# Changing the cost model of a software-scheduled transformer kernel: SyncE charges, GpSimd multiplies, gated PV terms and early fill

## The chip, the cores and the metric

The kernel runs on one core of one Trainium2 chip. The metric is the device time of one execution in microseconds (us), as the median of several executions. Smaller is better.

Names of engines, with what this kernel has them do: PE multiplies matrices, ScalarE (ACT) applies activation functions, VectorE (DVE) and GpSimd (POOL) do elementwise work, and SyncE (SP) issues the transfers, one after another: in the timeline of its queue after the change, from 626.17 to 633.66 us, each begins only when the one before it has ended.

## The reference, cut to what matters

```python
# S = 2048 tokens, D = 512, F = 1792, H = 32 heads of Dh = 16
def _A_ref(x, wqkv, wo):                      # attention
    qkv = ...; q, k, v = qkv[0], qkv[1], qkv[2]
    scores = jnp.einsum("bhqd,bhkd->bhqk", q, k) * Dh ** -0.5
    p = _softmax(scores, axis=-1)
    o = jnp.einsum("bhqk,bhkd->bhqd", p, v)
    return o.transpose(...).reshape(B, S, D) @ wo
def _B_ref(x, w1, w2):                        # feed-forward
    return _silu(x @ w1) @ w2
x = x + _A_ref(_layernorm(x), A_wqkv, A_wo);  x = x + _B_ref(_layernorm(x), B_w1, B_w2)
x = x + _A_ref(_layernorm(x), A_wqkv, A_wo);  x = x + _B_ref(_layernorm(x), B_w1, B_w2)
```

There are 32 heads with 2048 x 2048 scores in each of two layers, so the exponentials dominate: they take 1468.6 of the 1513.8 us for which ScalarE is busy (page below).

## The kernel before

The kernel is a stream of steps. Each step computes four 128x512 blocks of scores. ScalarE exponentiates three of them exactly (one activation of 512 columns and one of 1024), and VectorE and GpSimd approximate the fourth: VectorE converts the scores to a bit pattern (`d_y`), and GpSimd makes two more terms (`d_z`) from it. The rest, the *background* (projections, normalisations `xn`, feed-forward), is cut into parts, and a scheduler written in Python puts each part into a step where a model of the engines says it will fit without making ScalarE wait. The order of instructions on each engine is fixed when the kernel is built. A wrong number in the model is therefore never corrected at run time: it becomes a wait.

```python
class Model:                                   # (cut)
    GROUP = 0.217;  FIX = 0.69;  TRANSPOSE = 1.27;  TRANSPOSED = 1.7;  DMA = 0.64
    def transpose(self):                       # a transposing transfer on SyncE's queue
        self.sp = max(self.sp, self.dve + 0.1) + self.TRANSPOSE
        self.landed = self.sp + self.TRANSPOSED
    def fits(self, cost, landed=0.0):
        held, pe, dve, sums, _ = cost
        if landed > (self.pe if pe else self.dve):
            return False
        ...
```

A part names what it needs (`need=("xn", ...)`: one of three buffers that a transpose must have read; `need=("fT", L, c)`: transposed tiles), and the model's `landed` time decides when it may be placed. The feed-forward loads its weights two tiles ahead and names no need for them:

```python
    class W1:                                  # (cut)
        def get(self, ft):
            self.load(ft + 2)                  # one dma_start on SyncE; w1pool has 3 buffers
            if bg.model: bg.model.dma(1)
            return self.tiles.pop(ft)
```

The output of a head group is divided by its sum; where it came by a transposing transfer, both inputs are in SBUF. The model charges 0.43 us of VectorE time:

```python
        nc.vector.reciprocal(rec[:], att[:, :, :, 16:17])
        yield part(0.43, held=not by_dma(L, qc, pi, g, par))
        nc.vector.tensor_tensor(out=attn[L, qc]..., in0=att[:, :, :, 0:DH],
                                in1=rec[:].to_broadcast([P, 4, 4, DH]), op=ALU.mult)
```

*Fill* is matmul work without use (`zero` weights into an open accumulator, or `warm` into a free bank), put into PE's gaps and meant to keep its clock up, which in the trace of before fell to half after windows in which PE was busy for 2.13 and 1.00 of 3.4 us (windows view below).

The softmax here doesn't subtract the row's maximum and nothing guards it: scores larger than these inputs give would overflow.

## Time and profile before

| | before |
|---|---|
| median of 3 executions | 1565.61 us (1565.21 to 1566.28) |
| span of the profiled execution | 1562.4 us |
| before the first exponential | 14.1 us |
| stream of exponentials and tanhs, if ScalarE never waited | 1494.5 us |
| ScalarE's waits in the stream | 13.1 us |
| after the last exponential | 40.9 us |

The third to sixth rows are my own arithmetic on the trace: I took the ends of successive ScalarE activations. When nothing waits, an end follows the end before it by 490 ns (512 columns) or 917 ns (1024 columns); what is above that, counted where it exceeds 60 ns, is a stall. The four parts add up to the span within 0.3 us. (The prediction's 13.8 us also counts 0.65 us before the stream.)

First the page of the kernel before: the busy table, then two groups (line, engine, operation, output and inputs, count, busy us, mean ns, idle before it and its releaser).

```profile
PE 1474.8 (94%) x13400; PEld 468.1 (30%) x13400; DVE 1079.3 (69%) x1733; ACT 1513.8 (97%) x2191; POOL 1114.4 (71%) x1184
...
L1157 ACT ACTIVATE p_sb<-s_ps 128x512 bf16<-128x512 f32 x2026 | 1468.6, 1105 | 9.3 <-PE d_ps L925 8.2
...
L619 DVE TENSOR_TENSOR attn<-ot,rec 128x256 bf16<-128x256 bf16 x45 | 49.4, 1098 | 1.5
```

ScalarE is busy for 97% of the span, nearly all of it in exponentials. The mean of 1105 ns is not the time that one adds: activations overlap in the trace (2026 of 1105 ns are 2239 us, within 1468.6 us busy), which is why I used the ends. The VectorE multiply (the second group) has a mean of 1098 ns, where the model charges 430. The tile view of `attn` shows minimum, median and maximum in ns:

```profile
L619 DVE TENSOR_TENSOR attn<-ot,rec x45: 425/1274/1291, 235.6 to 1506.9; 128x256 bf16<-128x256 bf16 x45
...
L619 DVE TENSOR_TENSOR attn<-att,rec x19: 411/424/425, 172.2 to 1523.9; 128x256 bf16<-128x256 f32 x19
```

The same multiply takes 424 ns if one input is in PSUM (second line) and mostly 1274 ns if both are in SBUF (first line). Not always: seven of the 45 took 425 to 432 ns. In this trace, six of these began when at most 0.16 us was left of the GpSimd instruction that was running (a `d_z`), and one when GpSimd was idle; each of the other 38 ended 268 to 275 ns after the running `d_z` did. So in this trace the slow multiply ends with GpSimd's running instruction, as if it waited for it; it is not slow in itself.

The waits view of the kernel before (who waited for whom: us in total, times, longest) and its timeline near 250 us (start, us, engine, line, operation; in brackets the idle time before it and what ended it) belong together:

```profile
ACT p_sb L1157 <- PE d_ps L925: 8.2, 10, 3.0
...
PE d_ps L925 <- DVE d_y L1074: 7.1, 9, 3.1
...
DVE xn L414 <- DMA fT<-xn: 4.3, 2, 4.1
```

```profile
246.69 5.58 SPq L317 DMA_TRANSPOSE fT<-xn  x3
...
250.63 0.42 DVE L414 TENSOR_SCALAR xn<-x,mv,rstd 128x513 bf16<-128x513 bf16 x1 [4.13 <-DMA fT<-xn]
250.96 0.68 DVE L1074 TENSOR_SCALAR d_y<-d_ps 128x512 uint16<-128x512 f32 x1
251.70 0.37 PE L925 MATMUL d_ps<-QT,KT 32*128 32x512 bf16 x1 [3.15 <-DVE d_y L1074]
...
253.44 1.51 ACT L1157 ACTIVATE p_sb<-s_ps 128x512 bf16<-128x512 f32 x2 [3.00 <-PE d_ps L925]
```

VectorE could not write the normalised tile before 250.63, because SyncE's queue had not finished the transpose that reads its buffer. It held up the `d_y` behind it for 4.13 us, PE waited 3.15 us for that, and ScalarE resumed only at 253.44. With 1.0 us more in the half-clock spell that follows, this place costs ScalarE 4.1 us.

The last view that matters is the windows view of the kernel before: a stretch, its length, busy time of PE, its weight loads, VectorE, ScalarE and GpSimd (x instructions), then the granted PE clock (1.00 is full), DMA share and GB/s.

```profile
30.90:34.30 3.40, 2.13 (x18) 0.40 (x14) 3.34 (x9) 3.06 (x5) 1.29 (x4) 1.00 0.01 3
34.30:44.50 10.20, 8.45 (x45) 1.21 (x47) 7.06 (x14) 8.25 (x12) 6.97 (x8) 0.50 0.43 105
...
249.30:252.70 3.40, 1.00 (x13) 0.23 (x12) 1.61 (x3) 1.15 (x2) 0.00 (x0) 1.00 0.54 112
252.70:256.10 3.40, 3.40 (x20) 0.79 (x20) 1.60 (x4) 1.75 (x3) 2.09 (x2) 0.50 0.03 6
```

PE runs at half clock from 34.3 to 44.5 us and from 252.7 to 256.1 us. Before both, PE's work was thin: 2.13 of 3.4 us busy, and 1.00 of 3.4. Two further half-clock spells (stretches in which half the clock is granted), at 85.5 and 1051.5 us, are 3.4 us long.

### The profile page before, as it was taken

How to read it: one execution, taken by the hardware profiler on the slowest of the kernel's cores; microseconds unless marked ns; L12 is line 12 of the kernel's file. 1: busy time of each engine (PE TensorE's matmuls, PEld its weight loads, DVE VectorE, ACT ScalarE, POOL GpSimd, SP SyncE). 2: the span in 40 equal slices, each digit the busy share in tenths (PEclk: the TensorE clock that was granted, in tenths of full speed). 3: DMA queues.
4: the chain of work that ended last, by engine and by line, in shares of the span. 5: the costliest groups of instructions: out<-in, count | busy, mean ns of one | idle time of the engine just before them, and what ended most of it. 6: DMA issues, size and time to landing. Idle time of an engine off the chain costs nothing. (4 is left out here: it accounts for less than half of the span.)

```text
span 1562.4 us, 34354 instructions
## 1 busy us (share of the span) xinstructions
PE 1474.8 (94%) x13400; PEld 468.1 (30%) x13400; DVE 1079.3 (69%) x1733; ACT 1513.8 (97%) x2191; POOL 1114.4 (71%) x1184
## 2 busy tenths in 40 slices
PE   7999998899999999899998999998999899999998
PEld 3222332232322322222322323322332232222225
DVE  6877676667776777767776677676667666676645
ACT  6999998999999999999999999999999999999993
POOL 2888776677876778667876778776777677776760
PEclk9999999999999999999999999999999999999999
DMA  4110023101221112201122010121022101121110
GB/s 142 28 28 2 5 39 62 31 18 42 45 45 28 31 25 49 52 17 41 21 47 45 11 35 8 25 58 32 18 46 62 30 19 29 45 48 22 39 45 14
DMA packets 149443, 55.85 MB, mean 36 GB/s; under 512 B 127776, under 2 KB 148768, under 8 KB 149280
## 3 DMA queue, kind: packets, MB, share of 16 engines
q1 hardware_dynamic: 149280, 53.65, 15.0%
q8 instruction: 105, 1.72, 0.5%
q14 instruction: 58, 0.48, 0.1%
HBM read 28.57 MB, written 4.19 MB: 21 GB/s over the span
## 5 line engine op out<-in xcount | busy, mean ns | idle before, releaser
L1157 ACT ACTIVATE p_sb<-s_ps 128x512 bf16<-128x512 f32 x2026 | 1468.6, 1105 | 9.3 <-PE d_ps L925 8.2
L1074 DVE TENSOR_SCALAR d_y<-d_ps 128x512 uint16<-128x512 f32 x1012 | 696.9, 689 | 400.5 <-PE d_ps L925 359.5
L925 PE MATMUL s_ps<-QT,KT 32*128 32x512 bf16 x3084 | 629.8, 383 | 51.6 <-ACT p_sb L1157 38.8
L925 PE MATMUL d_ps<-QT,KT 32*128 32x512 bf16 x1012 | 390.1, 385 | 10.3 <-DVE d_y L1074 7.1
L925 PEld LDWEIGHTS <-KT 32*128 32x128 bf16 x4096 | 186.8, 91 | 639.9 <-issue 587.1
L949 PE MATMUL o_ps<-p_sb,VA 128*32 128x512 bf16 x3039 | 311.8, 388 | 8.2 <-DVE oB L1054 1.1
L949 PE MATMUL o_ps<-d_y,VA 128*32 128x512 f16 x1012 | 153.2, 379 | 0.0
L949 PEld LDWEIGHTS <-VA 128*32 128x32 bf16 x4096 | 86.7, 95 | 161.6 <-issue 123.8
L727 PE MATMUL f_ps<-w_sb,hT 128*128 128x512 bf16 x392 | 104.1, 382 | 0.0
L949 PEld LDWEIGHTS <-VB 128*32 128x32 f16 x2024 | 78.3, 98 | 55.6 <-issue 0.8
L949 PE MATMUL o_ps<-w_qkv,zero 128*32 128x512 bf16 x1344 | 93.1, 382 | 0.0
L665 ACT ACTIVATE t_sb<-h_ps 128x512 f32<-128x512 f32 x98 | 88.1, 899 | 0.0
L668 DVE SCALAR_TENSOR_TENSOR hT<-t_sb,h_ps 128x512 bf16<-128x512 f32 x98 | 67.2, 686 | 22.8 <-ACT t_sb L665 22.6
L619 DVE TENSOR_TENSOR attn<-ot,rec 128x256 bf16<-128x256 bf16 x45 | 49.4, 1098 | 1.5
L1054 DVE CAST oT<-o_ps 128x512 bf16<-128x512 f32 x64 | 43.5, 680 | 7.7 <-PE o_ps L949 7.7
L414 DVE TENSOR_SCALAR xn<-x,mv,rstd 128x513 bf16<-128x513 bf16 x64 | 41.6, 663 | 5.7 <-DMA fT<-xn 4.3
L403 DVE BATCH_NORM_STATS2 st<-x 128x6 f32<-128x512 bf16 x64 | 43.5, 680 | 2.0 <-DMA x<-in_A_x_dram 2.0
L727 PEld LDWEIGHTS <-hT 128*128 128x128 bf16 x392 | 29.3, 98 | 46.4 <-issue 25.0
L949 PEld LDWEIGHTS <-zero 128*32 128x32 bf16 x1344 | 25.5, 95 | 40.3 <-issue 28.1
L480 PE MATMUL k_ps<-xnT,w_qkv 128*128 128x512 bf16 x128 | 35.4, 389 | 1.6 <-DVE xnT L444 0.9
L480 PE MATMUL q_ps<-xnT,w_qkv 128*128 128x512 bf16 x136 | 36.6, 389 | 0.0
L407 POOL TENSOR_SCALAR rstd<-mv 128x2 f32<-128x2 f32 x32 | 7.7, 240 | 39.4 <-DVE mv L405 37.9
(2299 smaller groups left out, 2109.1 us busy)
## 6 DMA issues: line engine op xcount, KB each, us to landing
wo<-in_A_wo_dram SPq DMA_DIRECT2D x8, 512.0 KB, 3.7
QT<-q SPq DMA_DIRECT2D x240, 16.0 KB, 1.8
x<-in_A_x_dram SPq DMA_DIRECT2D x7, 512.0 KB, 4.3
out_dram<-x SPq DMA_DIRECT2D x16, 128.0 KB, 1.7
w_sb<-in_B_w_dram SPq DMA_DIRECT2D x1, 1792.0 KB, 12.4
w_qkv<-in_A_wqkv_dram SPq DMA_DIRECT2D x3, 512.0 KB, 5.8
w_tail<-in_B_w_dram SPq DMA_DIRECT2D x3, 512.0 KB, 5.2
ot<-oT SPq DMA_TRANSPOSE x45, 2.4
```

Of the source, the lines that this page charges most:

```text
L403: nc.vector.bn_stats(st[:], x_sb[c][:, i, :])
L414: nc.vector.tensor_scalar(out=wide[:].rearrange("p (a b) -> p a b", b=19), in0=x_wide[c][:, D * i : D * (i + 1) + 1], scalar1=mv[:, 0:1], ...
L480: nc.tensor.matmul(ps.rearrange("p (t q) -> p t q", q=P) if len(r.shape) == 3 else ps, lhsT=lhs(ct), rhs=r, start=(ct == 0), stop=(ct == C ...
L619: nc.vector.tensor_tensor(out=attn[L, qc][:, :, P * g : P * (g + 1)].rearrange("p t (j s) -> p t j s", s=32)[:, :, :, 16 * par : 16 * par ...
L665: nc.scalar.activation(t_sb, h_ps, ACT.Tanh, scale=0.5)
L668: nc.vector.scalar_tensor_tensor(out=hT[:, ft, :], in0=t_sb, scalar=1.0, in1=h_ps, op0=ALU.add, op1=ALU.mult)
L727: nc.tensor.matmul(y_ps, lhsT=hT[:, ft, tq * P : (tq + 1) * P], rhs=w2_sb[:, ft, :], start=(ft == 0), stop=(ft == FT - 1),)
L925: nc.tensor.matmul(out, lhsT=KT[L, kt // 4][r, g, (kt % 4) * P : (kt % 4 + 1) * P], rhs=QT[g][r, par, :], start=True, stop=True,)
L949: nc.tensor.matmul(o_tiles[key][32 * j : 32 * j + 32, :], lhsT=lhsT, rhs=rhs, start=(o_count[key][j] == 0), stop=stop,)
L1054: nc.vector.tensor_copy(out=o, in_=o_tiles[key][:])
L1074: nc.vector.tensor_scalar(out=pr["y"][:, len(pr["ds"]), :], in0=s_ps[:], scalar1=float(1024 * SCALE * math.log2(math.e)), scalar2=float(10 ...
L1157: nc.scalar.activation(p_sb, s_ps, ACT.Exp, bias=-SHIFT * math.log(2.0) + math.log(EXP_SUM), scale=float(SCALE),)
```

## The change: its intent and diff

The intent is to bring the model closer to the machine: every transfer occupies SyncE in the model, transposes land later, the slow multiply leaves VectorE, PV terms (products of the approximate terms with V) are not placed before GpSimd has made them by the model's clock, and the steps with thin PE work near the start get fill.

```diff
-    TRANSPOSED = 1.7
+    TRANSPOSED = 2.4
 ...
+    def load(out, in_):                       # replaces nc.sync.dma_start for x, wo, w1, stores
+        nc.sync.dma_start(out, in_)
+        if bg.model:
+            bg.model.dma(1)
 ...
-        yield part(0.43, held=not by_dma(L, qc, pi, g, par))
-        nc.vector.tensor_tensor(
+        if by_dma(L, qc, pi, g, par):
+            scale = nc.gpsimd.tensor_tensor
+            bg.model.scaled = bg.model.pool_busy(0.62)
+        else:
+            yield part(0.43, held=True)
+            scale = nc.vector.tensor_tensor
+        scale(
 ...                                           # out_proj:
+        bg.model.sp = max(bg.model.sp, bg.model.scaled)
 ...                                           # emit_pv, the PV terms:
-            while d["rhs"] and (must or d["rhs"][0][0] <= t):
+            while d["rhs"] and (
+                must or d["rhs"][0][0] <= t and (t < 8 * NKT or d["ready"][d["rhs"][0][1]] <= m.pe)
+            ):
 ...                                           # the early fill, in steps 9 to 12:
+                if t > 5 and m.free <= m.pe and bg.idle():
+                    n = int((m.sd - m.pe - 2 * m.SWITCH) / m.GROUP)
+                    if n > 0:
+                        warm(n)
+                        m.to("B")
+                        m.pe += m.GROUP * n
                 m.late_d()
                 emit_d(t, d_blks[0])
```

The order of instructions shows what the diff does not: 45 multiplies move to GpSimd, the early fill comes to nine matmuls (two, five and two in three steps), VectorE's order is the same up to about 200 us.

More of the change, by code (lines that the diff above doesn't have):

```diff
@@ L135, in __init__ @@
         self.mode = None
+        self.scaled = 0.0
         self.early = False
@@ L285 @@
     RUNS += [(1, qc, 0, ORDER, range(NKT)) for qc in range(2, NC)]
+    bg = Background()
     const = ctx.enter_context(tc.tile_pool(name="const", bufs=1))
@@ L328, in load_x @@
         for i in range(0, 4, n):
-            nc.sync.dma_start(x_sb[c][:, i : i + n, :], src[:, i : i + n, :])
+            load(x_sb[c][:, i : i + n, :], src[:, i : i + n, :])
     load_x(0, parts=2)
@@ L354 @@
     nc.scalar.activation(table[:, 0:32], zero[:], ACT.Exp)
-    bg = Background()
     xnT = {}
@@ L647, in load_wo @@
         wo[0] = hpool.tile([P, FT, 512], BF16, name="wo", tag="hT")
-        nc.sync.dma_start(wo[0][:, 0:CT, :], A_wo.rearrange("(ct p) e -> p ct e", p=P))
+        load(wo[0][:, 0:CT, :], A_wo.rearrange("(ct p) e -> p ct e", p=P))
     def out_proj(L, qc):
@@ L681, in ffn_out @@
         tt = 4 * c + i
-        nc.sync.dma_start(of[tt * P : (tt + 1) * P, :] if L == 1 else x1[c][:, i, :], x_sb[c][:, i, :])
+        load(of[tt * P : (tt + 1) * P, :] if L == 1 else x1[c][:, i, :], x_sb[c][:, i, :])
     class W1:
@@ L694, in load @@
                 self.tiles[ft] = w1pool.tile([P, CT, P], BF16, name="w1", tag="w1")
-                nc.sync.dma_start(
+                load(
                     self.tiles[ft][:],
@@ L701, in get @@
             self.load(ft + 2)
-            if bg.model:
-                bg.model.dma(1)
             return self.tiles.pop(ft)
@@ L1082, in emit_d @@
         d = dict(blk=blk, pair=len(pairs), left=NT)
+        d["ready"] = [m.dve + 0.1]
         d["rhs"] = [(t + 1, 0, pr["y"][:, len(pr["ds"]), :].bitcast(FP16))]
@@ L1101, in other_terms @@
             )
-            bg.model.pool_busy(bg.model.ADD[n])
+            ready = bg.model.pool_busy(bg.model.ADD[n])
             for i, d in enumerate(pr["ds"]):
                 d["rhs"].append((t + 3 + k, k + 1, z[:, i, :].bitcast(FP16)))
+                d["ready"].append(ready)
     def end_group(L, qc, pi, g, par):
```

## The prediction

> **What bounds the kernel.** ScalarE. In the busy table it is busy 1513.8 of 1562.4 us (97%); in the groups view nearly all of that is 2026 exponentials (1468.6 us), whose number, shapes and order the change leaves alone: it only moves seven tanhs by a few rows. From the timeline and the windows: about 14 us pass before the first exponential, ScalarE streams from there to about 1521, and the last 41 us (final projection and FFN, half ScalarE-idle) are a chain of PE, DVE and ScalarE that the diff does not touch. So only ScalarE stalls inside the stream can be won. Taking ends of successive exponentials from the trace (one step costs 490 + 917 ns when nothing waits), these stalls sum to only 13.8 us, 0.9%. A gain of 2% (31 us) is out of reach.
>
> **Where these 13.8 us lie, and what the change does to each.**
> 1. 249-256 us: 4.1 us. A VectorE normalisation (xn) waited 4.13 us for a buffer still being transposed by SyncE's queue (waits view), VectorE held up the approximate-score conversion, PE idled 3.15 us and its clock then halved for 3.4 us. Charging loads and stores to SyncE and 2.4 us for landing makes the scheduler place xn later. Gain about 4.
> 2. Eleven small stalls, 3.8 us together, follow within about 4 us of a head-output multiply on VectorE. That multiply takes 1.27 us (median of 45) where the model charges 0.43; the same multiply with a PSUM input takes 0.42. [...] Moving the 45 multiplies takes about 50 us off VectorE (1079 to about 1030)[...]. Gain about 3.5; this includes the clock drop at 1051 us (1.3 us).
> 3. 32-44 us: 3.0 us. PE is at half clock from 34.3 to 44.5 us. The new early fill is nine matmuls, about 2 us: two, five and two before three score matmuls. [...] the trace's half-clock spans are 3.4 and 10.2 us long, and begin after 3.4 us windows in which matmuls streamed only 26 to 43% of the time, while windows at 47% kept the clock. The fill lifts the window before 34.3 us to about 0.53. I expect the early drop to go; about 0.3 us per step of waiting for the approximate conversion stays. Gain about 2.
> 4. 85-90 us: 1.7 us. VectorE runs two slow xn (1.2 us each) in one step; VectorE's order is identical up to about 200 us. It stays, with its clock drop.
>
> Waiting for the modelled readiness of PV terms protects PE from the busier GpSimd and gains little by itself. New collisions (remaining xn bursts, GpSimd backlog after VB and rstd work) may cost about 1 us.
>
> **Predicted:** 1565.6 - 9 = 1556.5 us, range 1553 to 1562. Chances: faster by over 2% 0.005, within 2% 0.985, slower 0.01.
>
> **What would show it.** After: ScalarE busy unchanged at 1514; span about 1553; no half clock at 34-44, 252 and 1051 us, still one near 85; VectorE's wait for the transpose gone; VectorE about 1030[...]; prologue and last 41 us unchanged.
>
> **What would make it wrong.** The GpSimd multiply taking well over 1 us and delaying PV terms until PE waits; pushed-back background work piling up before a deadline; a new clock drop; the clock windows falling elsewhere in time.

The terms are gains of 4, 3.5, 2 and 0 us less about 1 us for new collisions: 8.5 us, put as 9. The term of 3.5 us stands on the stalls in the trace, that of 2 us on the windows in the trace.

## More of the kernel before

Runs sent together ran on the same chip and shared their executions of the kernel before; runs 1 to 4, runs 5 to 8 and runs 9 to 12 were three such jobs, on three chips, so kernels of different jobs are compared by their ratios to the kernel before.

## The result and the profile after

| | before | after |
|---|---|---|
| median of 6 executions | 1565.58 us | 1561.16 us |
| range | 1564.36 to 1567.12 | 1558.93 to 1565.79 |
| span of the profiled execution | 1562.4 | 1557.2 |
| ScalarE's waits in the stream | 13.1 | 7.8 |

The ratio is 0.9975, with a 95% interval from 0.9958 to 0.9992. Here and below, a ratio is the mean time of one kernel's fast executions over that of the other's in the same rounds, so not quite the ratio of the medians quoted. The gain is 3.9 us, less than half of the 9 predicted. And the times now spread over 7 us.

The trace comes from the fastest execution, 1558.93 us. In it the gain is 5.2 us. The busy table of the page after, and the tile view of `attn` (minimum, median and maximum in ns):

```profile
PE 1470.4 (94%) x13299; PEld 475.7 (31%) x13397; DVE 1035.2 (66%) x1688; ACT 1512.9 (97%) x2191; POOL 1138.8 (73%) x1229
```

```profile
L631 POOL TENSOR_TENSOR attn<-ot,rec x45: 617/621/622, 237.2 to 1503.3; 128x256 bf16<-128x256 bf16 x45
```

The load of ScalarE (1512.9 us) and of VectorE (1035.2) is as predicted. GpSimd is busy for 1138.8 us, up from 1114.4, and a multiply on it takes 0.62 us, as the changed model charges. So the waits must tell. The waits view of after:

```profile
ACT p_sb L1172 <- PE d_ps L936: 2.7, 4, 0.9
...
ACT t_sb L678 <- PE h_ps L487: 1.9, 2, 1.1
PE h_ps L487 <- DMA w_10625<-in_B_w_dram: 1.9, 1, 1.9
...
PE h_ps L487 <- DMA w_7458<-in_B_w_dram: 1.6, 1, 1.6
```

The 4 us wait for the transposed buffer is gone, and ScalarE's waits for `d_ps` fell from 8.2 to 2.7 us. But matmuls of the feed-forward now wait for weight tiles, 1.9 and 1.6 us, and ScalarE's tanh (`t_sb`) waits for them. The timeline at the larger of the two, first SyncE's queue, then PE and ScalarE:

```profile
626.17 5.55 SPq L538 DMA_DIRECT2D QT<-q  x8
631.82 1.22 SPq L320 DMA_TRANSPOSE ot<-oT  x1
633.08 0.58 SPq L325 DMA_DIRECT2D w_10625<-in_B_w_dram  x1
```

```profile
635.73 1.04 PE L487 MATMUL h_ps<-fT,w_10625 128*128 128x512 bf16 x4 [1.87 <-DMA w_10625<-in_B_w_dram]
...
636.81 0.60 ACT L678 ACTIVATE t_sb<-h_ps 128x512 f32<-128x512 f32 x1 [1.06 <-PE h_ps L487]
...
637.04 0.62 PE L960 MATMUL o_ps<-p_sb,VA 128*32 128x512 bf16 x4
```

The tile `w_10625` is needed at about 634 us and is issued only at 633.08, because eight copies of Q (5.55 us) and a transpose stand before it in the queue. PE waits 1.87 us, ScalarE 1.06 us. After that the matmuls take about 0.6 us instead of 0.4: the clock has dropped. The windows view of after shows this spell and an earlier one:

```profile
36.20:39.60 3.40, 2.27 (x18) 0.44 (x18) 3.15 (x7) 2.74 (x5) 0.97 (x3) 1.00 0.48 84
39.60:46.40 6.80, 6.45 (x40) 1.14 (x37) 3.38 (x6) 5.41 (x8) 5.52 (x7) 0.50 0.24 79
633.50:637.00 3.50, 1.63 (x10) 0.48 (x9) 0.84 (x2) 2.44 (x4) 1.38 (x2) 0.99 0.57 125
637.00:640.30 3.30, 3.30 (x24) 0.83 (x20) 2.09 (x4) 2.98 (x5) 2.17 (x3) 0.50 0.17 40
```

The second line is the spell that the early fill was to prevent. It came anyway, 5 us later and 6.8 us long. Stalls by stretch, from the ends of activations, in us:

| stretch | before | after, this trace | predicted change |
|---|---|---|---|
| below 50 us (in the stream) | 3.33 | 3.99 | -2 |
| 80 to 95 us | 1.68 | 1.05 | 0 |
| 230 to 300 us (transposed buffer, two multiplies) | 4.91 | 0.00 | about -5 |
| 400 to 700 us | 1.20 | 2.71 | small gains, about 1 lost |
| all others | 2.00 | 0.07 | about -2 |

### The profile page after: what moved, and what is told of

Same layout as the page of the kernel before. It is cut to its first block, busy times and chain, and to the rows that moved or that the text cites. A ratio compares the mean times of both kernels' runs of the same rounds, so it can differ in the third digit from the quotient of the medians.

```text
span 1557.2 us, 34303 instructions
## 1 busy us (share of the span) xinstructions
PE 1470.4 (94%) x13299; PEld 475.7 (31%) x13397; DVE 1035.2 (66%) x1688; ACT 1512.9 (97%) x2191; POOL 1138.8 (73%) x1229
## 5 line engine op out<-in xcount | busy, mean ns | idle before, releaser
L936 PE MATMUL s_ps<-QT,KT 32*128 32x512 bf16 x3084 | 648.5, 381 | 52.0 <-ACT p_sb L1172 37.2
L936 PEld LDWEIGHTS <-KT 32*128 32x128 bf16 x4096 | 193.1, 91 | 650.2 <-issue 602.1
L738 PE MATMUL f_ps<-w_sb,hT 128*128 128x512 bf16 x350 | 97.1, 382 | 3.9 <-issue 3.2
L487 PE MATMUL v_ps<-w_qkv,xnT 128*128 128x512 bf16 x112 | 33.0, 382 | 1.4 <-issue 0.6
```

Source lines behind the costliest of these rows:

```text
L487: nc.tensor.matmul(ps.rearrange("p (t q) -> p t q", q=P) if len(r.shape) == 3 else ps, lhsT=lhs(ct), rhs=r, start=(ct == 0), stop=(ct == C ...
L738: nc.tensor.matmul(y_ps, lhsT=hT[:, ft, tq * P : (tq + 1) * P], rhs=w2_sb[:, ft, :], start=(ft == 0), stop=(ft == FT - 1),)
L936: nc.tensor.matmul(out, lhsT=KT[L, kt // 4][r, g, (kt % 4) * P : (kt % 4 + 1) * P], rhs=QT[g][r, par, :], start=True, stop=True,)
```

## The experiments

**Theory A**: the two terms that work gain 4.1 and 3.8 us as predicted, but the rearranged queue brings late weight loads, and the early fill gains nothing; with these, half-clock spells come or do not come with the phase of clock windows. **Theory B**: the busier GpSimd delays PV terms and gives the gain back. **Theory C**, formed after the first four runs: background work is now placed before what it needs has landed.

Theory A speaks of a phase because of the clock records. In the trace of before the half-clock spells of the stream last 10.240 us and three times 3.413 us, in that of after 6.827 and 3.413 us; in all traces each is one, two or more times 3.413 us long. In each trace all changes of the clock lie on one grid of 3.413 us, within 3 ns, and the grid lies elsewhere in each trace (one point of it is at 34.280 us from the start of the span in the trace of before, one at 39.626 us in that of after, which is 1.57 steps of the grid later). What sets the grid is not shown. From the traces I computed the activity in each step of the grid (a *window*) as the share of the array at work: a matmul counts its streaming time times the share of rows and columns that it uses. The streaming time is my estimate, in proportion to the columns streamed: for 512 columns 1% less than 215 ns, the least distance between the starts of the five fill matmuls of the trace of after (215 to 227 ns apart at full clock). A score matmul uses 32 rows where the fill uses 128 (`32*128` and `128*128` in the timelines) and counts a quarter. Over the fourteen traces (windows from 18 to 1520 us at full clock):

```
windows followed by half clock:      53, activity 0.03 to 0.366, and one (of the 53) at 0.388
windows followed by full clock:    6010, activity from 0.377 up, and three at 0.355, 0.359, 0.366
the same by "any matmul running":  drops up to 0.537, kept from 0.398  (32 drops lie above 0.398)
```

The share of the array divides the windows far better than whether a matmul runs. Some matmul records are missing from the traces (98 of 13397 in the trace of after). That makes the computed activity too low, so it could explain the three kept windows, but not the drop at 0.388; that one stays unexplained.

In the expectations the runs go by labels: again (1), nofill (2), w1ahead (3), multonly (4), noready (5), land17 (6), chargeonly (7), gapfill (8), nofill_w1 (9), gap_noready (10), gap_nomult (11), gap2_xn (12). The profiles of runs 9 to 12 were taken again later: their kept traces are of executions of 1554.8, 1556.0, 1578.9 and 1566.9 us span. Numbers below, and the table above, are from the kept traces; the quoted lines of runs 11 and 12 are from the first profiles.

### 1. The changed kernel again

No edit.

> The changed kernel once more, for a second trace and more times. Theory A (the shortfall is two late weight loads and half-clock spells that come or not with the phase of 3.4 us clock windows): times spread over about 1558.5 to 1566 us, falling with the mean granted clock of the run (0.997 near 1559, 0.991 near 1565); PE again waits over 1.5 us twice for a w1 tile, near 445 and 633 us; the half-clock spells sit at other places than in the first trace, but only after windows in which less than about 0.37 of the array worked. Theory B (the scatter is something in the queues, not the clock): times do not order by the granted clock.

Measured: median 1561.45 us (1559.15 to 1565.36), ratio 0.9985 [0.9972, 0.9998]. The six executions with their mean granted clock, and those of the first measurement:

```
again: 1559.15 0.997 | 1560.04 0.997 | 1561.00 0.996 | 1561.89 0.995 | 1564.96 0.991 | 1565.36 0.990
after: 1558.93 0.997 | 1559.74 0.997 | 1560.01 0.997 | 1562.32 0.995 | 1564.32 0.991 | 1565.79 0.991
```

The times order by the clock. In this trace the early spell did not occur (stalls below 50 us: 2.44 us), but both late weight loads were followed by one (400 to 700 us: 5.62 us). Theory A holds for the scatter. Four of these twelve executions are as slow as before the change.

### 2. Without the early fill

```diff
-                if t > 5 and m.free <= m.pe and bg.idle():
-                    n = int((m.sd - m.pe - 2 * m.SWITCH) / m.GROUP)
-                    ...                       # the whole fill block
```

> The changed kernel without its early fill (nine matmuls taken out, nothing else). My prediction gave the fill 2 us of gain, so this would be 2 us slower than the changed kernel. Theory A: the fill does not keep the clock and holds up ScalarE by about 0.6 us in the first trace, so this is equal or up to 1 us faster; ScalarE's stalls between 30 and 47 us sum to about 3.0 us, as before, against 3.7.

Measured: 1560.79 us (1559.49 to 1565.11), ratio 0.9980 [0.9968, 0.9992]; stalls below 50 us 3.34 us, as before. It is not 2 us slower, so the fill does not gain what I gave it. By the ratios it is 0.8 us faster than the changed kernel in the same job, but the intervals overlap.

### 3. Weight tiles loaded three ahead

```diff
-    w1pool = ... tc.tile_pool(name="w1pool", bufs=3)
+    w1pool = ... tc.tile_pool(name="w1pool", bufs=4)
-            for ft in range(2): self.load(ft)
+            for ft in range(3): self.load(ft)
-            self.load(ft + 2)
+            self.load(ft + 3)
         # (and two buffers instead of three for the tiny tile "rec", to make room)
```

> The changed kernel with w1 tiles loaded three ahead instead of two (one buffer more). Theory A: PE's waits for w1 tiles and the stalls near 447 and 635-641 us (0.9 and 1.8 us in the first trace) go, and with them two chances of a half-clock spell; 2.5 to 4 us faster than the changed kernel, and less scatter between executions. Theory B: the stalls stay or move, the gain is under 1 us.

Measured: 1558.72 us (1557.65 to 1560.42), ratio 0.9963 [0.9951, 0.9975]: by the medians 2.7 us faster than the changed kernel in the same job (3.4 us by the ratios). The waits view has no line for a weight tile left, and stalls from 400 to 700 us are 0.00. The late weight loads were a cause, and the scatter fell with them from 6.2 to 2.8 us.

### 4. Only the multiply moved

Edit: the kernel before, with the multiply's hunk and its `scaled` lines alone.

> The kernel before with only the head-output multiply moved to GpSimd (with its modelled time). If the multiplies on VectorE cost what I read (3.8 us with their clock spell): 3 to 4.5 us faster than before, stalls after a reciprocal gone; the wait for a transposed buffer at 250 us stays unless the schedule shifts. Rival: GpSimd at 73% delays its terms and gives half of it back: under 2 us.

Measured: 1567.93 us (1566.03 to 1572.70), ratio 1.0024 [1.0013, 1.0036], so 3.7 us *slower* than before. Both expectations failed: I had expected a gain of 3 to 4.5 us, the rival under 2 us. From its waits view:

```profile
PE k_ps L481 <- DMA xnT<-xn: 3.9, 4, 1.4
...
DVE xn L415 <- DMA fT<-xn: 3.3, 1, 3.3
```

PE waits for transposed tiles (`xnT`) and VectorE for a transposed buffer. No line shows PE waiting more than 0.3 us for GpSimd's terms. Of the 4.2 us by which this trace is longer than that of before, 2.7 us are stalls in the stream and 1.6 us come after it, with a half-clock spell at 1536 us. My reading: the multiply no longer takes VectorE's time in the model, so background work is placed earlier, ahead of transfers whose landing the old model puts too early (after 1.7 us; in the trace of before the transposes of `attn` landed a median of 2.5 us after their issue). This is theory C; run 6 tests it.

### 5. Without the rule for PV terms

```diff
-                must or d["rhs"][0][0] <= t and (t < 8 * NKT or d["ready"][d["rhs"][0][1]] <= m.pe)
+                must or d["rhs"][0][0] <= t
```

> The changed kernel without the rule that a PV term waits for its modelled time on GpSimd. If the slower multiply-only run is due to GpSimd delaying PV terms (theory B), this loses about 3 us against the changed kernel and PE's waits for GpSimd's terms appear. If it is due to background matmuls placed before their transposes or weights have landed (theory C), the rule is worth under 1 us and PE waits on GpSimd for less than 0.5 us in all, as in the other traces.

Measured: 1563.88 us (1561.26 to 1566.08), ratio 0.9994 [0.9982, 1.0006]. PE's waits for GpSimd are 0.3 us in all. By the ratios it is 1.4 to 3.0 us slower than the changed kernel, but both scatter by 5 us or more with the clock, so this alone decides nothing (run 10 does). With the clock at 0.991 its trace is, however, what the slow executions of the changed kernel look like: PE's list of operations and tiles is the same in both, only which PV term takes which place differs, and that only after step 128. The windows view and, from PE's timeline, the five fill matmuls of this kernel:

```profile
28.40:31.80 3.40, 1.93 (x19) 0.50 (x17) 3.39 (x8) 3.40 (x6) 0.93 (x2) 1.00 0.00 0
31.80:48.80 17.00, 15.58 (x71) 2.35 (x74) 9.57 (x19) 10.57 (x16) 8.26 (x11) 0.50 0.28 64
```

```profile
35.98 2.31 PE L769 MATMUL warm<-w_qkv,ident 128*128 128x512 bf16 x5
```

The same five in the timeline of the changed kernel, at full clock:

```profile
34.56 1.25 PE L769 MATMUL warm<-w_qkv,ident 128*128 128x512 bf16 x5
```

Here a window ended before the fill came, the clock halved at 31.8 us, and these five then took 2.31 us with ScalarE waiting behind them. The spell lasted 17 us; stalls below 50 us are 7.59 us, against 3.3 without fill. Another spell, at 1533.7 us, makes the end 1.7 us longer (42.6 against 40.9 us). Together that is 5.3 us above the trace of after, and 1558.93 + 5.3 = 1564.2 us is where its slow executions begin. (No slow execution of the changed kernel was profiled, so this is an inference.)

### 6. Transposes landing after 1.7 us again

```diff
-    TRANSPOSED = 2.4
+    TRANSPOSED = 1.7
```

> The changed kernel with the landing time of a transpose back at 1.7 us (the traces show a median of 2.5 us). Theory C: matmuls again wait for transposed tiles (xnT, fT), as in the multiply-only run, 1 to 3 us slower than the changed kernel. Theory B: no difference, within 1 us.

Measured: 1565.33 us (1563.30 to 1569.05), ratio 1.0008 [0.9996, 1.0020]; by the ratios 3.6 to 5.2 us slower than the changed kernel, about all of its gain. From its waits view, the waits for transposed tiles that are back:

```profile
PE k_ps L487 <- DMA xnT<-xn: 3.0, 4, 1.1
```

This trace also has a long early spell (stalls below 50 us are 7.56 us) and one after the stream, as that of run 5, so its length alone proves nothing. But at the same granted clock the loss remains: the executions of this kernel at 0.996 took 1563.3 and 1563.8 us, that of the changed kernel 1561.0 us (run 1). Theory C holds: without the longer landing time, the moved multiply and the other parts gain nothing. Whether multiply and landing time alone would do was not run.

### 7. Only the charges and the landing time

Edit: the kernel before, with `load()` and `TRANSPOSED = 2.4` alone.

> The kernel before with only the charges to SyncE and the 2.4 us landing. My prediction gives this part 4 us: the 4 us stall at 250 us goes and the eleven stalls after VectorE multiplies stay. Theory A adds that the schedule then puts w1 loads behind eight Q copies and a transpose in SyncE's queue, so that a wait of 1.5 to 2 us for a w1 tile appears near 450 and 637 us: net gain 1 to 4 us on before. If that wait is absent, the multiply or the rule for PV terms makes it.

Measured: 1569.51 us (1568.38 to 1574.20), ratio 1.0035 [1.0023, 1.0047], 5.4 us *slower* than before. The 4 us stall at 250 us is gone and a wait for a weight tile (2.1 us) has come, as expected. But the net gain of 1 to 4 us did not: stalls within 7 us after a multiply on VectorE rose from 11 (3.8 us) to 24 (10.8 us). In the new order the unmodelled 0.85 us of the multiply meets other VectorE work more often, and nine half-clock spells stand in its stream, against four before.

### 8. Fill in a gap that is certain

In three early steps PE waits for VectorE before the fourth score (0.57 us at full clock in the traces of before, after and run 2). This kernel is run 3 without the early fill, and with two fill matmuls there.

```diff
             for i in range(n1):
+                if i == 1 and t >= 10:
+                    warm(2)
                 score(a_blks[i], s1[i])
```

> The changed kernel with w1 tiles three ahead, its early fill taken out, and instead two fill matmuls in each of three steps in the gap of 0.57 us in which PE waits for VectorE before the fourth score. Theory A: the gap is free, the clock spell at 32-44 us goes in most executions, ScalarE's stalls from 30 to 47 us fall from 3.0-3.7 us to 1.0-1.8; 1 to 2.5 us faster than w1ahead, about 1557. If fill cannot keep the clock here, the same as w1ahead.

Measured: 1557.34 us (1556.83 to 1557.43), ratio 0.9953 [0.9941, 0.9965]. The fill in the timeline, between the third and the fourth score:

```profile
34.91 0.58 PE L936 MATMUL s_ps<-QT,KT 32*128 32x512 bf16 x3
...
35.42 0.61 PE L769 MATMUL warm<-w_qkv,ident 128*128 128x512 bf16 x2
...
36.05 0.37 PE L936 MATMUL s_ps<-QT,KT 32*128 32x512 bf16 x1
```

The scatter is now 0.6 us. But the spell came, at 37.2 us and 6.8 us long; stalls from 30 to 47 us are 2.5 us instead of the 1.0 to 1.8 expected (2.77 us below 50 us). In this trace the gap fill moves the spell and does not remove it: in the next steps, too, PE waits for VectorE (0.52 us at 38.56 us and 0.35 us at 39.92 us).

### 9. Neither fill

Edit: run 8 without its six fill matmuls.

> The gapfill kernel without its six gap matmuls (so: the changed kernel, w1 three ahead, no early fill). If the gap fill itself is what wins against w1ahead, this is 1 to 1.5 us slower than gapfill with early stalls of about 3.3 us; if taking out the harmful early fill is enough, it equals gapfill within 0.6 us.

Measured: 1558.26 us (1555.80 to 1560.20), ratio 0.9951 [0.9934, 0.9968]; stalls below 50 us are 4.11 us, with a spell of 13.7 us from 33.8 us. The ratio is that of run 8, so the gap fill's effect on the mean is not shown. The range is 4.4 us here, against 0.6 in run 8 and 2.3 in run 10, which also has the gap fill; with five or six executions each, that it narrows the range is likely but not shown.

### 10. The rule for PV terms taken out, with little scatter

Edit: run 8 with the edit of run 5.

> The gapfill kernel without the rule that PV terms wait for their modelled time. In this kernel, which scatters by only 0.6 us, the rule's own worth shows. PE never waited for GpSimd's terms in the noready trace, so theory C: within 0.7 us of gapfill. Theory B: 2 us or more slower, with PE waits for GpSimd.

Measured: 1555.84 us (1555.17 to 1557.49), ratio 0.9938 [0.9924, 0.9952], the fastest kernel. It is not within the 0.7 us of run 8 that I expected (2.3 us faster by the ratios), but the interval overlaps run 8's, so a gain is not shown. A loss of 2 us is excluded: theory B falls.

### 11. The multiply back on VectorE

Edit: run 8 with the lines of before for the multiply.

> The gapfill kernel with the 45 head-output multiplies back on VectorE. From the stalls after these multiplies in the trace of before (3.8 us) and in the charge-only trace: 3.5 to 8 us slower than gapfill, multiplies near 1.27 us and stalls with clock spells after them. If the multiply's place no longer matters, within 1 us.

Measured: 1581.45 us (1578.30 to 1583.54), ratio 1.0100 [1.0082, 1.0117], by the ratios about 23 us slower than run 8, far more than expected. The multiplies take 1278 ns again (median). From the waits view:

```profile
ACT p_sb L1167 <- PE d_ps L931: 14.9, 32, 1.1
...
PE d_ps L931 <- DMA QT<-q: 4.2, 1, 4.2
```

In the kept trace 27 stalls, 13.7 us together, stand within 7 us after a multiply. 8.7 us more come from one place near 985 us, where a projection of Q is forced at its deadline and PE waits for its copies (4.2 us in the line above). My reading, which no run isolates: with the multiply on VectorE and every transfer charged, background work is pushed back until it collides.

### 12. More gap fill, and a dearer normalisation

```diff
                 for blk in d_blks:
+                    if 13 <= t <= 15:
+                        warm(2)
                     emit_d(t, blk)
-                yield part(0.45, need=("xn", ...))
+                yield part(0.8, need=("xn", ...))
```

> Gapfill with two more fill matmuls in each of the next three steps, where PE also waits for VectorE, and 0.8 us instead of 0.45 charged for a normalisation (traces: 0.4 to 1.2 us), which spreads the two that stand in one step near 81 us. Expected: the stall of 1.7 us near 85 us gone, the early ones down from 2.8 to about 1.5 us, clock kept: 1.5 to 3 us faster than gapfill, about 1555. If the new schedule collides elsewhere, equal to gapfill or slower.

Measured: 1566.81 us (1566.38 to 1568.71), ratio 1.0010 [0.9995, 1.0024], by the ratios about 9 us slower than run 8. The stall near 85 us is gone, as expected. But stalls below 50 us rose to 6.36 us, with the added fill at half clock from 39 us on, and a projection of Q now stands at its deadline, near 975 us, where PE waits for its copies and ScalarE loses 8.7 us (waits view):

```profile
PE d_ps L936 <- DMA QT<-q: 4.5, 1, 4.5
```

## Why the prediction was wrong, point by point

The range held the median, but of the 9 us of gain forecast only 3.9 came. Two terms were wrong: the early fill (step 3), which failed, and the allowance for new collisions, which was too small.

- *"Only ScalarE stalls inside the stream can be won", 13.8 us at most.* Right. In every trace the span is start, 1494.5 us, stalls and end.
- *Step 1, the transposed buffer, "gain about 4".* Right in the changed kernel: 4.1 us, gone in both traces.
- *Step 2, the multiplies, "gain about 3.5".* Right in size in the changed kernel (3.8 us); on GpSimd a multiply took 0.62 us. Yet neither step gains by itself (runs 4 and 7: 3.7 and 5.4 us slower). I added up parts that only work together; that both came out at their size in the changed kernel was luck.
- *Step 3, the early fill, "gain about 2".* This step failed. I measured activity by whether any matmul was running, 0.43 in the window before the spell, took the place of the windows from one trace, and concluded that two matmuls would do. By the share of the array it is 0.23. In three of the five traces with this fill (runs 3, 5 and 6) the window that dropped ended at 31.8 to 32.4 us, before the first recorded fill matmul (32.7 to 33.1 us). In the trace of after the fill kept the window before 36.2 us (0.453), but brings the next one, to 39.6 us, only to 0.352, within the range where the traces drop. Only in run 1 did all windows stay above, the lowest at 0.387, and no early spell came. Stalls below 50 us became 3.99, 2.44, 7.59, 7.56 and 4.80 us in these five traces (after, runs 1, 5, 6 and 3), mean 5.3, against 3.33 to 4.11, mean 3.6, in the five without any fill (before, runs 2, 4, 7 and 9). So in the traces the term was about -1.6 us, not +2. The times put the loss at 0.8 us (run 2) and 1.9 us (run 9 against run 3, by the ratios), with intervals that overlap: that the fill gains 2 us is excluded or nearly so, that it costs time is likely.
- *"New collisions ... may cost about 1 us".* Mis-sized. Late weight tiles cost 2.7 us in the first trace and 5.6 us in the second; run 3 took them away and won 2.7 us. My list of collisions named normalisations and GpSimd, and not the one transfer whose landing no part waits for in the model. With the traces' sizes the sum comes out: 4.1 + 3.8 - 1.6 - 2.7 is 3.6 us, where 3.9 was measured; the agreement is rough, for the parts are not independent.
- *"Waiting for the modelled readiness of PV terms ... gains little by itself".* Right (run 10).
- *"No half clock at 34-44 and 1051 us".* Wrong for the first, right for the second. *"One near 85"*: wrong in the trace of after (full clock from 46.5 to 637.0 us), where the stall near 87 us stayed, 1.05 us, without a spell; right in run 1 (84.4 us). It comes and goes between the traces.
- *"The clock windows falling elsewhere in time"* was on my list of dangers, and I gave it no size. It goes with the 5 us between fast and slow executions of one kernel, whose times order by the clock. The stalls that I read were one execution's draw.

What stays open: how much of run 7's loss is spells and how much is VectorE alone, what the charges to SyncE are worth without the longer landing time (they were never run apart), and whether run 10 is truly faster than run 8.

## What to carry to other kernels

In a statically scheduled kernel, corrections to the cost model need not be additive: correcting one number can move work against the next wrong one, so build and measure the combinations, and see that the model knows the landing of every transfer that work depends on. No fill was shown to gain time here; placed by an estimate it became a wait itself, and it took 2.31 us instead of 1.25 just when the clock had dropped. Where a trace is one draw from a phase lottery, compare the granted clocks of all executions before you size a term from one trace.
